# Block sums of the weights made by GpSimd in the front, and the second pair's first layer at two levels of Strassen

## The chip, the cores and the metric

The kernel runs on one core of a Trainium2 chip. A core has five engines with queues of their own: TensorE (PE, the matmuls, with PEld for its weight loads), VectorE (DVE), ScalarE (ACT), GpSimd (POOL) and SyncE (SP, which here only issues DMAs). Each takes its instructions in a fixed order and waits for semaphores of the others. Operands lie in SBUF, the on-chip memory of 128 partitions, matmul results in PSUM, in eight banks. Everything is computed in float32. The metric is the device time of one execution in microseconds.

## The reference

Two blocks follow each other. The first is linear attention with decay, in blocks of 64 positions, for 4 batches, 8 heads, 768 positions and 64 channels. Its result, with heads put beside each other, is `x` of 4 x 768 x 512. The second block mixes by a Fourier transform and adds a network of two layers:

```python
X = np.fft.fft(np.fft.fft(x, axis=1), axis=2)
u = x + np.real(X)
un = (u - mean(u)) / np.sqrt(var(u) + 1e-06)      # over the 512 channels
out = u + np.maximum(un @ w_ch1, 0.0) @ w_ch2     # 512 -> 2048 -> 512
```

The weights `w_ch1` and `w_ch2` are inputs, so whatever is made from them is made in every execution.

## The kernel before, in words

**Two stages.** In the front, batches go one after another through attention (`attn`, six chunks of 128 positions for each batch), the folds and matmuls of the Fourier transform and the normalisation (`fft_ln`). The transform uses its symmetries: VectorE adds and subtracts rows and mirrored rows (`fold_x`, `fold_a`, `fold_b`), TensorE multiplies the folded rows by small tables (L516, then `width`, L528 to L533), and `norm` makes the normalised tile. The mirrored rows come by indirect DMAs (gathers) that GpSimd issues in `mirror_a` and `mirror_b` (L439, L445, L452). GpSimd also scales keys (`kd`, L270) and the attention state (`st`, L319), takes the inverse root of the variance (`rs`, L550), and issues the indirect stores of rows to the output (L624).

A group is two tiles of 128 positions; there are twelve. The first four (`PLAIN`) go through both layers as plain matmuls, `mlp` (L635 and L649), woven between the front's work. The other eight (`LATE`) are transposed in blocks by VectorE into a tile with the tag `e` (L576), written to device memory (`utd`) and computed after the front, in four pairs of two groups each, with Strassen's method in Winograd's form: a product of 2 x 2 blocks with seven block products (`PRODUCTS`, L678) instead of eight. At two levels each of the seven is again made from seven products of quarters, 49 in all.

**The late stage.** Before it, VectorE makes the first level's block sums of both weights (`combine_weights`). `late` then runs the pairs in order. A first layer at one level is `first_layer` (L882, 7 x 8 x 2 matmuls with 256 columns), one at two levels is `deep_first` (L967, 49 x 4 matmuls with 128 columns). The second layer has two levels in every pair (`deep_second`, L1037). `DEEP` (L767) says how many pairs have a first layer at one level: two. At two levels a product needs block sums of a quarter of the weights: three or four tiles of 128 x 512, for each of seven weight blocks of either layer. GpSimd makes them while the one-level first layers run: `keep_sums` under pair 0 (those of the second weight, T1, T2, T4; the fourth is made in place of a quarter) and `keep_sums_w` under pair 1 (those of the first weight, S1 to S4). SP stores them in device memory (`s2.td`, `s2.sd`), and `load_three` brings three back ahead of each product. The tag `tx` with six slots holds a sum on its way out as well as on its way back. `place_sums_w` puts the fourth sum of each block of the first weight over a quarter that is no longer needed. In pair 0, `prepare_b` has the loads for the first two products issued behind the sums of the last turn, i = 6.

**What sets the order.** A planner in the compiler orders the instructions of each engine by program order and by when it takes their operands to be ready; it allots slots of a tag too. Program order comes from Python generators: each piece of work yields its estimated length, and `weave` draws from a second generator as much as a ratio allows. The last weave of the front takes the rest of `fr` (from batch 2's Fourier matmuls on, then batch 3) as its lead and the plain matmuls `back` beside it. `tc.keep_in_program_order` pins an instruction behind the one traced before it on its engine; instructions that are not pinned may step ahead. The front's tiles lie in pools that are closed after it, and the late stage's tiles are laid over them; of these `e` has two slots of 2 KB per partition.

In `in_step` the seven steps of each product alternate with those of the next, so that a product's end is interleaved with the start of the one behind.

## Time and profile before

| what | value |
|---|---|
| time, median of 3 runs | 798.99 us (798.94 to 800.15) |
| time of the profiled execution | 798.86 us |
| its span in the profile | 796.9 us |
| TensorE busy | 766.8 us, 96% |
| VectorE busy | 587.7 us, 74% |
| GpSimd busy | 195.6 us, 25% |
| sums by GpSimd under pair 0 | 433.08 to 471.83 us, 28 instructions |
| sums by GpSimd under pair 1 | 524.67 to 563.5 us, 28 instructions |
| pair 0, first layer from; second layer from | 428.71; 476.28 us |
| pair 1, first layer from; second layer from | 521.84; 568.46 us |
| pair 2, first layer from | 611.34 us |
| pair 3, first layer from | 698.88 us |

All times inside an execution count from the start of its span. A line of a group or of the timeline names the start, the duration, the engine, the line of the kernel, the operation, the tile written and those read, and in brackets the idle time ahead of it with what ended it. Matmuls in float32 have two records each. "SPq" is the queue of SP, a time there that of issuing DMAs.

### The profile page before, as it was taken

The page shows a single profiled execution, that of the slowest core. Times are in us where ns is not written, and L with a number is a line of the kernel's source. Part 1 is how long each engine was busy: PE and PEld are TensorE (multiplying, and loading weights), DVE is VectorE, ACT ScalarE, POOL GpSimd, SP SyncE. Part 2 cuts the span into 40 slices and gives each one's busy share as a digit, 9 for nine tenths or more (in the row PEclk, how much of TensorE's full clock was granted, in tenths as well). Part 3 has the DMA queues.
Part 4 walks back from the last instruction along what each step waited for, and adds up shares of the span by engine and source line. Part 5 has one row for each costly group of instructions (what it writes and reads, how often), then busy time and mean ns, then how long its engine had stood idle before and what let it go on. Part 6 is the DMA issues. An engine that isn't in the chain of part 4 may idle for free.

```text
span 796.9 us, 14576 instructions
## 1 busy us (share of the span) xinstructions
PE 766.8 (96%) x5616; PEld 647.2 (81%) x5616; DVE 587.7 (74%) x1148; ACT 216.7 (27%) x512; POOL 195.6 (25%) x196
## 2 busy tenths in 40 slices
PE   6989999999999999999999999999999999999996
PEld 5768776858675766777956889998999999999995
DVE  6899889685853573246598998769977699758983
ACT  3755443324431221221200221012210442024300
POOL 3233231011101020121003960279204101230021
PEclk9999999999999999999999999999999999999999
DMA  9979624238842037443232375345954555455432
GB/s 241 260 152 253 179 84 130 92 58 215 206 131 87 27 79 144 103 132 106 47 71 89 138 239 170 95 167 190 326 170 145 165 175 178 129 177 187 125 121 79
DMA packets 152331, 116.80 MB, mean 147 GB/s; under 512 B 113998, under 2 KB 113998, under 8 KB 152262
## 3 DMA queue, kind: packets, MB, share of 16 engines
q1 hardware_dynamic: 147120, 103.39, 46.1%
q0 software_dynamic: 2112, 6.69, 2.5%
q10 hardware_dynamic: 3030, 5.78, 2.1%
q8 instruction: 45, 0.74, 0.4%
q14 instruction: 24, 0.20, 0.1%
HBM read 83.58 MB, written 32.25 MB: 145 GB/s over the span
## 4 chain that ended last, share of the span: by engine, by line
PE 77%; DVE 10%; DMA 6%; issue 4%; ACT 2%; POOL 1%; SPq 0%; POOLq 0%; ACTq 0%; DVEq 0%
PE p L1037 21%; PE p L882 12%; PE p L967 11%; PE pm L649 9%; PE pm L635 8%; PE pa L516 3%; PE pa L332 3%; PE pa L298 3%; DMA raw<-in_moe_w_ch_dram 2%; DMA x<-xb,ix 2%; PE pa L328 2%; PE pa L274 1%; PE pa L315 1%; PE pa L348 1%; PE pa L279 1%
## 5 line engine op out<-in xcount | busy, mean ns | idle before, releaser
L635 PE MATMUL pm<-ut,w 128*128 128x256 f32 x512 | 118.8, 381 | 0.0
L649 PE MATMUL pm<-w,hr 128*128 128x512 f32 x256 | 115.7, 596 | 0.1
L635 PEld LDWEIGHTS pm<-ut,w 128*128 128x128 f32 x512 | 94.5, 190 | 14.0 <-issue 2.1
L649 PEld LDWEIGHTS pm<-w,hr 128*128 128x128 f32 x256 | 46.6, 190 | 49.3 <-issue 48.0
L1051 POOL TENSOR_TENSOR y<-y,u 128x512 f32<-128x512 f32 x12 | 18.8, 1570 | 199.1 <-DVE y L1060 156.7
L1037 PE MATMUL p<-tx,sx 128*128 128x128 f32 x416 | 54.9, 275 | 0.0
L1037 PEld LDWEIGHTS p<-tx,sx 128*128 128x128 f32 x416 | 50.6, 192 | 0.0
L882 PE MATMUL p<-ur,w 128*128 128x256 f32 x192 | 46.9, 379 | 0.1
L270 POOL TENSOR_TENSOR kd<-k,decay 128x512 f32<-128x512 f32 x20 | 22.2, 1109 | 95.9 <-PE pa L315 58.0
L1045 DVE TENSOR_TENSOR y<-p,y 128x128 f32<-128x128 f32 x92 | 25.6, 286 | 22.4 <-PE p L1037 15.7
L1043 ACT COPY y<-p 128x128 f32<-128x128 f32 x48 | 12.8, 266 | 104.1 <-PE p L1037 103.8
L882 PEld LDWEIGHTS p<-ur,w 128*128 128x128 f32 x192 | 36.3, 190 | 5.7 <-issue 0.5
L302 DVE TENSOR_TENSOR sc<-pa,decay 128x512 f32<-128x512 f32 x48 | 31.5, 683 | 8.5 <-PE pa L298 8.2
L1037 PE MATMUL p<-w,ha 128*128 128x128 f32 x288 | 37.4, 275 | 0.0
L298 PEld LDWEIGHTS pa<-qT,kT 64*128 64x128 f32 x384 | 26.0, 193 | 13.2 <-ACT qT L281 7.2
L1037 PEld LDWEIGHTS p<-w,ha 128*128 128x128 f32 x288 | 35.0, 192 | 0.2
L332 PE MATMUL pa<-sc,v 128*64 128x128 f32 x384 | 31.5, 282 | 3.8 <-DVE sc L302 3.7
L643 ACT ACTIVATE hr<-pm 128x256 f32<-128x256 f32 x44 | 16.7, 384 | 65.9 <-PE pm L635 65.6
L298 PE MATMUL pa<-qT,kT 64*128 64x128 f32 x384 | 30.7, 292 | 3.2 <-ACT qT L281 2.9
L549 POOL TENSOR_SCALAR ve<-mv 128x2 f32<-128x2 f32 x12 | 3.4, 286 | 122.6 <-DVE mv L546 122.6
L882 PE MATMUL p<-sx,w1s 128*128 128x256 f32 x128 | 32.9, 380 | 0.2 <-DVE sx L785 0.2
L332 PEld LDWEIGHTS pa<-sc,v 128*64 128x64 f32 x384 | 23.1, 137 | 11.4 <-DVE sc L302 5.3
(227 smaller groups left out, 1717.4 us busy)
## 6 DMA issues: line engine op xcount, KB each, us to landing
tx<-td SPq DMA_DIRECT2D x84, 256.0 KB, 2.9
raw<-in_moe_w_ch_dram SPq DMA_DIRECT2D x32, 512.0 KB, 5.4
tx<-sd SPq DMA_DIRECT2D x42, 256.0 KB, 2.7
sd<-tx SPq DMA_DIRECT2D x28, 256.0 KB, 2.0
k<-in_k_dram SPq DMA_DIRECT2D x24, 256.0 KB, 5.0
q<-in_q_dram SPq DMA_DIRECT2D x24, 256.0 KB, 6.0
v<-in_v_dram SPq DMA_DIRECT2D x24, 256.0 KB, 4.4
td<-tx SPq DMA_DIRECT2D x21, 256.0 KB, 2.0
```

The source lines that it names most:

```text
L270: nc.gpsimd.tensor_tensor(kd, kt, kpow, op=ALU.mult)
L298: mm(pss[hi][:, hp, :], lhsT=kT[HD[hi], hp, :], rhs=qT[HD[hi], hp, :], start=True, stop=True)
L302: nc.vector.tensor_tensor(t, pss[hi], decay[:, hi::2, :], op=ALU.mult)
L332: mm(po[HD[hi], hp, :], lhsT=vt[:, 2 * hp + hi, :], rhs=sc[hi][:, hp, :], start=(c == 0 and hp == 0), stop=(hp == HP - 1), skip_group_chec ...
L516: mm = nc.tensor.matmul(ps[:, n, :], lhsT=piece(a, i, n), rhs=cs[0:rows, a, i in (2, 3), n, :], start=(a == 0), stop=(a == 1))
L635: nc.tensor.matmul(ps, lhsT=w1[:, c, 128 * fc:128 * fc + 128], rhs=ut[:, c, :], start=(c == 0), stop=(c == KO - 1))
L649: nc.tensor.matmul(ps, lhsT=hr[(fc - f0) // 4][:, fc % 4, 128 * i:128 * i + 128], rhs=w2[:, fc, :], start=(fc == f0), stop=(fc == f1 - 1))
L882: nc.tensor.matmul(ps, lhsT=s2.A[a][:, kt, 128 * i:128 * i + 128], rhs=U[b][:, kt, :], start=(first and kt == 0), stop=(kt == 1), skip_gro ...
L967: nc.tensor.matmul(ps[:, 128 * i:128 * i + 128], lhsT=ab[m][0][:, 128 * i:128 * i + 128], rhs=ab[m][1], start=(start and i == 0), stop=Tru ...
L1037: nc.tensor.matmul(ps[:, 0:HM // 2], lhsT=ab[m][0][i], rhs=ab[m][1][:, i, :], start=(start and i == 0), stop=(i == HF // 2 - 1), skip_grou ...
L1045: V.tensor_tensor(o, ps[:, 0:HM // 2], o, op=ADD)
L1051: nc.gpsimd.tensor_tensor(o, y, u, op=ADD)
```

## The change

The sums of the weight blocks no longer hang on which first layer is running. One generator, `block_sums`, makes the four sums of a block and stores them.

For six blocks that are plain quarters of the weights and need no `combine_weights` (three of either layer: products 0, 1 and 5 of the first, 0, 1 and 6 of the second), `early_sums` makes them in the front: 24 instructions of GpSimd, each pinned, each followed by a store through SP to device memory. Three of the four tiles of a block take slots of `e`, and one a slot of its own, `ss`. `with_steps` puts one in wherever the last weave's lead has advanced by a 26th of its estimated length, at most one for each yield; what is left runs at the end. For the fourth sum of three blocks of the second weight, `place_sums_b` copies it from device memory into its place at the start of pair 0's first layer.

The other eight blocks (`later_sums`, 32 instructions) are made under pair 0's first layer: one block in each of the turns i = 0 to 5, two in the last, i = 6. With them, `DEEP` becomes 1, so that pair 1's first layer is computed at two levels. The keys' and queries' transposed tiles, `kT` and `qT`, get one buffer instead of two.

```diff
-        kT = new(at, [128, HP, C], "kT", bufs=2)
+        kT = new(at, [128, HP, C], "kT")
...
-        qT = new(at, [128, HP, C], "qT", bufs=2)
+        qT = new(at, [128, HP, C], "qT")
...
-    def keep_sums(k):
...
-    def keep_sums_w(k):
...
+    def block_sums(layer, k, quarters, shape, stage):
+
+        Q11, Q12, Q21, Q22 = quarters
+        S3, S2, S1, S4 = [stage[i](shape) if callable(stage[i]) else stage[i] for i in range(4)]
+        d = (s2.sd, s2.td)[layer][k] = [dram.tile(shape, F32, name=f"{'st'[layer]}d{k}{i}") for i in range(4)]
+        if layer == 0:
+            todo = ((3, S3, Q11, Q21, SUB), (1, S2, Q22, S3, SUB), (0, S1, S2, Q11, ADD), (2, S4, Q12, S2, SUB))
+        else:
+            todo = ((3, S3, Q22, Q12, SUB), (1, S2, S3, Q11, ADD), (0, S1, Q22, S2, SUB), (2, S4, Q21, S2, SUB))
+        for i, o, x, y, op in todo:
+            tc.keep_in_program_order(nc.gpsimd.tensor_tensor(o, x, y, op=op))
+            if o is not Q12:
+                nc.sync.dma_start(d[i], o)
+            yield 1.0
...
+    def early_sums():
...
+        blocks = [(0, 0, w1[:, k1, f1]), (1, 0, w2[:, b1, c1]), (0, 1, w1[:, k2, f1]), (1, 1, w2[:, b2, c1]),
+                  (0, 5, w1[:, k2, f2]), (1, 6, w2[:, b2, c2])]
+        for layer, k, t in blocks:
+            for d in block_sums(layer, k, (quarters_w, quarters_b)[layer](t), SHAPES[layer],
+                                [lambda s: new(ep, s, "e")] + [ep.tile(SHAPES[layer], F32, tag="ss", bufs=1, name=f"ss{layer}{k}")]
+                                + 2 * [lambda s: new(ep, s, "e")]):
+                yield d
...
+    def later_sums(i):
+
+        for layer, k in (((1, 3),), ((1, 2),), ((1, 4),), ((1, 5),), ((0, 3),), ((0, 4),), ((0, 2), (0, 6)))[i]:
+            q = (quarters_w, quarters_b)[layer]((s2.A, s2.B)[layer][PRODUCTS[k][layer]])
+            run(block_sums(layer, k, q, SHAPES[layer], [q[1] if layer else stage_tx] + 3 * [stage_tx]))
+
+    def place_sums_b():
+
+        for k in (0, 1, 6):
+            nc.sync.dma_start(quarters_b(s2.B[PRODUCTS[k][1]])[1], s2.td[k][3])
...
-    DEEP = 2
+    DEEP = 1
...
-            if j < min(DEEP, 2) and i < len(PRODUCTS):
+            if i < len(PRODUCTS):
                 if i == 0:
+                    place_sums_b()
                     tc.keep_in_program_order(nc.gpsimd.tensor_copy(s2.begun, h["a11"][:, 0, 0, 0:1]))
-                (keep_sums, keep_sums_w)[j](i)
+                later_sums(i)
...
+    def with_steps(gen, steps, each):
+
+        t = 0.0
+        for d in gen:
+            t += d
+            if t > each and next(steps, None):
+                t -= each
+            yield d
+        run(steps)
...
-    run(weave(fr, back, (t_back - t_half) / (t_rest - t_rest * t_half / t_back)))
+    t_last = t_rest - t_rest * t_half / t_back
+    run(weave(with_steps(fr, early_sums(), t_last / 26.0), back, (t_back - t_half) / t_last))
```

More of the change, by code (lines that the diff above doesn't have):

```diff
@@ L709, in quarters_b @@
         return [t[:, i:i + HF // 2, m:m + HM // 2] for i in (0, HF // 2) for m in (0, HM // 2)]
-    s2.td = []
+    s2.td, s2.sd = {}, {}
     s2.begun = wt.tile([128, 1], F32, name="begun")
-    def keep_sums(k):
-        pin = tc.keep_in_program_order
-        B11, B12, B21, B22 = quarters_b(s2.B[PRODUCTS[k][1]])
-        pin(nc.gpsimd.tensor_tensor(B12, B22, B12, op=SUB))
-        T1, T2, T4 = t = [new(s2.yp, [128, HF // 2, HM // 2], "tx", bufs=6) for _ in range(3)]
-        s2.td.append([dram.tile([128, HF // 2, HM // 2], F32, name=f"td{k}{i}") for i in range(3)])
-        for i, o, x, y, op in ((1, T2, B12, B11, ADD), (0, T1, B22, T2, SUB), (2, T4, B21, T2, SUB)):
-            pin(nc.gpsimd.tensor_tensor(o, x, y, op=op))
-            nc.sync.dma_start(s2.td[k][i], o)
@@ L725 @@
-    s2.sd = []
     def quarters_w(t):
         return [t[:, k, f:f + FH // 2] for f in (0, FH // 2) for k in range(2)]
-    def keep_sums_w(k):
-        pin = tc.keep_in_program_order
-        A11, A12, A21, A22 = quarters_w(s2.A[PRODUCTS[k][0]])
-        S3, S2, S1, S4 = [new(s2.yp, [128, FH // 2], "tx", bufs=6) for _ in range(4)]
-        s2.sd.append([dram.tile([128, FH // 2], F32, name=f"sd{k}{i}") for i in range(4)])
-        for i, o, x, y, op in ((3, S3, A11, A21, SUB), (1, S2, A22, S3, SUB), (0, S1, S2, A11, ADD), (2, S4, A12, S2, SUB)):
-            pin(nc.gpsimd.tensor_tensor(o, x, y, op=op))
-            nc.sync.dma_start(s2.sd[k][i], o)
+    def block_sums(layer, k, quarters, shape, stage):
[11 more added lines that the diff above has]
+            yield 1.0
@@ new lines @@
+    SHAPES = ([128, FH // 2], [128, HF // 2, HM // 2])
+    def early_sums():
+        k1, k2, f1, f2 = slice(0, 2), slice(2, 4), slice(0, FH), slice(FH, DFF)
+        b1, b2, c1, c2 = slice(0, HF), slice(HF, FO), slice(0, HM), slice(HM, DM)
+        blocks = [(0, 0, w1[:, k1, f1]), (1, 0, w2[:, b1, c1]), (0, 1, w1[:, k2, f1]), (1, 1, w2[:, b2, c1]),
[5 more added lines that the diff above has]
+                yield d
@@ new lines, in stage_tx @@
+    def stage_tx(shape):
+        return new(s2.yp, shape, "tx", bufs=6)
+    def later_sums(i):
[5 more added lines that the diff above has]
+            nc.sync.dma_start(quarters_b(s2.B[PRODUCTS[k][1]])[1], s2.td[k][3])
@@ L1139, in late @@
     def late():
-        for j in range(PAIRS):
-            if j < DEEP:
-                open_pair(j)
-                if j == 0:
-                    run(inputs(0))
-                first_layer(j)
-                if j + 1 < DEEP:
-                    in_step(second_layer(j) + [(inputs(j + 1), iter(()))])
+        open_pair(0)
+        run(inputs(0))
+        first_layer(0)
         in_step(second_layer(DEEP - 1) + [w for j in range(DEEP, PAIRS) for w in deep_pair(j)])
```

## The prediction

> **What bounds the kernel now.** I read the busy shares first, then the chain of waits, then the timelines of VectorE (DVE), GpSimd (POOL), TensorE (PE) and the DMA queue SP around the places that the change touches. On the page's first part:

> ```profile
> PE 766.8 (96%) x5616; PEld 647.2 (81%) x5616; DVE 587.7 (74%) x1148; ACT 216.7 (27%) x512; POOL 195.6 (25%) x196
> ```

> TensorE is the limit: some 30 us idle, two thirds of it at the two ends. Whatever makes it wait in between is paid in full, since its order is fixed. The chain of waits (start, us, what) of the last stage:

> ```profile
> 476.28 0.67 PE p L1037 x6
> ...
> 521.84 46.62 PE p L882 x216
> 568.46 0.67 PE p L1037 x6
> ...
> 611.34 0.89 PE p L967 x8
> ...
> 698.88 0.89 PE p L967 x8
> ```

> Read it as a calendar: second layer of pair 0 from 476.28, first layer of pair 1 (one level, L882) from 521.84, its second layer from 568.46, first layer of pair 2 (two levels, L967) from 611.34, of pair 3 from 698.88. Nothing but TensorE stands on the chain here.

> What the sums cost their neighbour shows in VectorE's timeline, during GpSimd's sums and after them:

> ```profile
> 437.11 1.48 DVE L896 TENSOR_TENSOR hs<-sv,ha 128x256 f32<-128x256 f32 x1
> 438.51 1.49 DVE L897 TENSOR_TENSOR hs<-ha,sv 128x256 f32<-128x256 f32 x1
> 439.92 0.41 DVE L894 TENSOR_TENSOR ha<-p,ha 128x256 f32<-128x256 f32 x1
> ...
> 478.38 0.42 DVE L896 TENSOR_TENSOR hs<-sv,ha 128x256 f32<-128x256 f32 x1
> ```

> The same operation takes 0.42 us alone and 1.48 beside a sum; L894, which reads PSUM, is untouched. So each sum holds one VectorE operation with two SBUF inputs by about 1.07 us. 28 sums run from 433.08 to 471.83: 1.384 us each.

> Then the place where GpSimd is idle and VectorE feeds TensorE directly (timelines of POOL, DVE, PE):

> ```profile
> 365.00 0.95 POOL L452 DMA_INDIRECT x<-xb,ix  x1 [0.30 <-issue]
> 389.11 0.22 POOL L549 TENSOR_SCALAR ve<-mv 128x2 f32<-128x2 f32 x1 [23.16 <-DVE mv L546]
> ...
> 370.08 0.42 DVE L475 TENSOR_TENSOR fe<-fe 128x256 f32<-128x256 f32 x1
> ...
> 370.56 0.59 PE L516 MATMUL pa<-cs,fe 128*128 128x193 f32 x2 [1.45 <-DVE fe L475]
> ```

> Eight folds of batch 3, all SBUF-only, run back to back from 367.18 to 370.50, and TensorE already waits 1.45 us for the last. GpSimd is free from 365.95 to 389.

> [...] the 256 KB stores of sums took 2.0, their loads 2.7 to 2.9.

> **Part 1, pair 1 at two levels.** From pair 0's second layer to pair 2's first layer now: 611.34 - 476.28 = 135.06. After: the stretch that leads from a second layer into a two-level first layer, 611.34 - 568.46 = 42.88, then a whole two-level pair, 698.88 - 611.34 = 87.54; together 130.42. Gain 4.64. In matmuls: one level issues 224 records at about 0.216 us (48.4), two levels 392 at 0.1117 (43.8). Its loads, its GpSimd inputs and `place_sums_w` come in the pattern that pair 2 shows behind pair 1, without a wait of TensorE.

> **Part 2, sums under pair 0's first layer.** 32 instead of 28: 433.08 + 32 x 1.384 = 477.4 instead of 471.8. Queue SP has the stores ahead of the loads of the second layer's T blocks:

> ```profile
> 468.84 3.33 SPq L723 DMA_DIRECT2D td<-tx  x3
> 472.26 2.79 SPq L759 DMA_DIRECT2D tx<-td  x6
> ```

> With the last store at about 477.8 the first load goes at 478.1 and lands at 480.8 to 481 (2.7 to 2.9), while TensorE wants T2 at 479.69 (first L1037 with tx). I take 1.2 us; ends 0 (a load put ahead of the stores) and 3 (the slowest landing, 5.5). VectorE ends four sums later, four times 1.07 behind; S2, now ready at 474.6, has 5 us of cover, S1 and S4 as much. `place_sums_b`'s three DMAs go at about 431, hidden behind 45 us of matmuls. Pair 1's 28 sums are gone, but TensorE lost nothing to them.

> **Part 3, 24 sums in the front.** Their GpSimd time, 24 x 1.3 = 31 us, fits into its idle time; their 24 stores too (DMA 30 to 40% busy, 2.0 us each). What counts is when they meet VectorE. A sum is pinned behind the GpSimd instruction before it in program order and behind nothing else. One step is due every 99.3/26 = 3.82 units. Summing the yields from batch 2's DFT on (where this weave starts): sums 1 to 5 fall in batch 2's DFT and norms, 6 to 15 in batch 3's attention, 16 right behind its last gathers, six (17 to 22) on the 21.6 units (1 + 3 + 9 + 5 x 1.4 + 1.6) before its first norm, 23 and 24 behind its first two norms' rs.
> - Batch 2, sums 1 and 2 right behind the gather of 263.24, mostly done when the folds begin at 266.56: 0.5 us (0 to 2.1).
> - Batch 2, sums 3 and 4 behind rs at 281.5 and 288.4, when VectorE turns to un. VectorE is gapless but for its waits on rs, up to sc, and TensorE waits 1.69 us for sc at 295.00. 2 x 1.07 = 2.1; I take 2.0 (0 to 3.2).
> - Attention of batch 3: VectorE's operations read PSUM; kd and st have 3 to 4 us until their matmuls. 0 (to 2).
> - Batch 3, sums 16 to 22: nothing but the staging slots spaces them, so they run from 366.0 as a bunch, over the folds. 16 is done when data lands at 367.15; 17 to 20 alternate with folds; 21 waits for 19's slot. Five of 17 to 22 before L475: 5 x 1.07 = 5.4 (2.1 with two, 7.5 with seven).
> - Sums 23 and 24: VectorE 2.1 later, against 2.02 us that it waits for TensorE at 428.9 after combining the weights: 0.3 (0 to 2.5).

> - Queues: the 24 stores take SP 24 x 0.36 = 9 us over 130 us. Behind a store that waits for its sum stand loads of q, k, v and stores of normalised tiles; SP is idle 30 of the 35 us before 386.8 and loads lead by a chunk, so 0. On TensorE everything behind L516 waits with it: the plain matmuls L635 stand in its order and can't step ahead, which is why 5.4 us of VectorE become 5.4 us of the kernel. Their cover would be an order in which some 25 of these records (0.216 us each) stood ahead of L516.

> kT and qT with one buffer cost nothing: in every chunk TensorE does L274, L279, then L298, so a chunk's copies come after the matmuls that read the one before. If chunks overlapped, a copy (0.59 us) would be waited for in each of 24. The buffers of the front lie 4 KB lower per partition and `ur` over another tile, so its load, now issued at 358, may wait longer; it is wanted at 428.7, and lands in 4 to 6: 0.

> Sum: 1.2 + 0.5 + 2.0 + 5.4 + 0.3 = 9.4 lost, 4.6 won: +4.8. Against the profiled execution (span 796.9, time 798.86) the span becomes 801.7 and the time 803.7; the median of the runs, 798.99, is 0.1 above that execution. I say 803.7.

> **Rivals.**
> - The bunch misses the folds (faster). One mechanism: the staging slots "e" are freed late enough to hold sums 17 to 22 until after 377, or the planner puts TensorE's plain matmuls ahead of L516. For it: six sums on two slots and one; against it: a slot comes back 2.3 us after its sum. Front 0, T2 1.2, gain 4.6: 795.5. It decides from where the front's losses fall under 3.4.
> - Cancelled: two or three sums meet the folds and the norms' cost half: 2.7 + 1.0 + 0.5 + 1.2 - 4.6 = +0.8, about 799.7. For it: VectorE's order may shift.
> - The slots block the queue: a sum without a slot holds up kd, st, rs behind it on GpSimd; the normalised tiles share "e", and SP issues stores in order, 12.8 us apart between its loads at 317.15 and 329.95. Two chunks late by 2 to 3 us each on top of +4.8: about 809. Against it: 3.82 units between sums there.
> - That pair 1 isn't computed at two levels: the code leaves no room; L967 would lack its 392 records.

> **Chances.** As forecast (801 to 807) 0.52; blocked queue 0.20; cancelled 0.14; faster 0.14. A measurement of this kernel tells about 0.2% (1.6 us) from no change. Faster 0.14, same 0.14, slower 0.72. The range 796 to 810 leaves out the best of the faster case (0.07) and the worst of the blocked one (0.1).

> **What would show it.** POOL sums bunched at the folds before the first norm of batch 3; folds of 1.4 us there; TensorE waiting about 7 us on L475 where it waited 1.45; pair 1 in 87.5 us; a wait of about 1 us for T2 in pair 0's second layer. Wrong if the folds stay at 0.42 us, if TensorE enters pair 0 less than 3.4 us later than 428.7, or if a new wait shows in the two-level pairs.

## The result, and the profile after

The changed kernel takes 819.73 us (median of 6 runs, 816.34 to 821.94) where the kernel before takes 799.12 beside it: a ratio of 1.0244, with a 95% interval of 1.0216 to 1.0272. The profiled execution has a span of 818.4 us, 21.5 more than before. The forecast of 803.7 had the right sign and under a quarter of the loss; its range ended at 810.

The page of the changed kernel: busy times, then the granted TensorE clock in 40 slices of 20.5 us.

```profile
PE 772.5 (94%) x5784; PEld 656.8 (80%) x5784; DVE 597.3 (73%) x1139; ACT 224.1 (27%) x512; POOL 202.3 (25%) x205
PEclk9999999999999699999899999999999999999998
```

TensorE has 168 records more, as forecast for one more first layer at two levels (392 against 224), and is idle 46 us instead of 30. The second row shows what the prediction has no term for: a slice with 0.6 of the full clock, from 266 to 286 us, and one with 0.8, from 389 to 409. In the kernel before each of the 40 shows a 9.

The chain of waits of the late stage (start, us, what):

```profile
503.26 1.92 PE p L902 x4
505.18 41.29 PE p L1058 x362
546.47 0.89 PE p L988 x8
...
634.01 0.89 PE p L988 x8
...
721.56 0.89 PE p L988 x8
```

Pair 1's first layer now has two levels (L988 from 546.47), and it and its second layer take 634.01 - 546.47 = 87.54 us, to the hundredth what the prediction read from pair 2. TensorE enters pair 0 at 451.20 instead of 428.71: the front alone lost 22.49 us. Ahead of 503.26 stands a stop of 2.88 us that the kernel before doesn't have; TensorE's timeline names what ended it:

```profile
503.26 1.92 PE L902 MATMUL p<-sx,w 128*128 128x256 f32 x4 [2.88 <-DVE ha L935]
```

Where the front lost its time: first the timelines of VectorE and TensorE in the kernel before at batch 2's second fold, then those of GpSimd, VectorE and TensorE in the changed one:

```profile
267.77 0.41 DVE L429 TENSOR_TENSOR fe<-fe 65x255 f32<-65x255 f32 x1
...
268.92 3.24 PE L516 MATMUL pa<-cs,fe 65*128 65x193 f32 x16 [0.33 <-DVE fe L470]
272.00 2.13 PE L516 MATMUL pa<-cs,fo 65*128 65x193 f32 x12
```

```profile
264.06 1.27 POOL L728 TENSOR_TENSOR e<-ss,w 128x512 f32<-128x512 f32 x1
270.80 2.80 POOL L728 TENSOR_TENSOR e<-w,ss 128x512 f32<-128x512 f32 x2
...
267.64 1.96 DVE L429 TENSOR_TENSOR fe<-fe 65x255 f32<-65x255 f32 x1
272.36 1.52 DVE L471 TENSOR_TENSOR fe<-fe 65x257 f32<-65x257 f32 x1
...
272.49 1.65 PE L516 MATMUL pa<-cs,fe 65*128 65x193 f32 x4 [4.04 <-DVE fe L470]
278.62 4.07 PE L516 MATMUL pa<-cs,fo 65*128 65x193 f32 x12
```

Six sums run from 264.06 to 273.6, and four fold operations take 1.5 to 2.0 us instead of 0.41. L516 comes at 272.49 instead of 268.92. And then twelve records of L516 take 4.07 us; before they took 2.13. The windows answer why (busy times of the engines; the number behind POOL's is the granted clock):

```profile
272.00:287.00 15.00, 14.05 (x54) 13.46 (x55) 5.08 (x12) 3.45 (x10) 1.60 (x2) 0.57 0.11 41
392.00:397.00 5.00, 5.00 (x15) 4.46 (x14) 5.00 (x15) 0.20 (x1) 0.00 (x0) 0.50 0.02 3
```

TensorE is busy nearly all the time, at half its rate. By 289.29, where the kernel before was at 279.79, the loss has gone from 3.57 to 9.50. The granted clock is at 0.50 from 271.35, inside the stop of 4.04 us, to 285.00, so it comes back only 12.5 us after the stop. Shorter stops bring it too (1.61 us in e18, below).

The other two places, in the timelines of SP, GpSimd, VectorE and TensorE; the first line is SP's load of the same `k` in the kernel before:

```profile
329.95 0.37 SPq L263 DMA_DIRECT2D k<-in_k_dram  x1
...
354.42 0.34 SPq L730 DMA_DIRECT2D sd<-e  x1
354.85 0.39 SPq L263 DMA_DIRECT2D k<-in_k_dram  x1
...
360.25 0.66 PE L274 MATMUL pa<-ident,k 128*128 128x128 f32 x4 [1.99 <-DMA k<-in_k_dram]
...
385.72 2.49 POOL L728 TENSOR_TENSOR e<-w,ss 128x512 f32<-128x512 f32 x2
386.74 2.03 DVE L426 TENSOR_TENSOR fe<-x,x 128x512 f32<-128x512 f32 x1 [3.46 <-DMA x<-xb,ix]
...
391.45 1.66 PE L516 MATMUL pa<-cs,fe 128*128 128x193 f32 x4 [5.51 <-DVE fe L475]
```

In batch 3's attention SP waits with the store of a sum until that sum is made, and the load of `k` stands behind it; before, it went out at 329.95. TensorE waits 1.99 us for it, and 3.55 us with the waits for `q` and those of the next chunk. At batch 3's fold the stop on L475 is 5.51 us instead of 1.45, and the half rate follows again.

The front's 22.5 us in the order of time:

| piece | us | read from |
|---|---|---|
| batch 2's second fold | 3.6 | L516 at 272.49 against 268.92 |
| half rate after it | 5.9 | 289.29 against 279.79, less the 3.57; a second wait of 0.46 is in it |
| batch 2's norms | 1.9 | L332 at 306.35 against 295.00, less the 9.50 |
| waits for `k` and `q` | 3.6 | 1.99 + 0.35 + 0.52 + 0.69 |
| batch 3's fold | 4.1 | 5.51 against 1.45 |
| half rate after it | some 3 | 0.50 from 391.45 to 397.64: half of these 6.2 us |

### The profile page after: what moved, and what is told of

Its sections match the earlier page's. It is cut to its first block, busy times and chain, and to the rows that moved or that the text cites. A ratio compares the mean times of both kernels' runs of the same rounds, so it can differ in the third digit from the quotient of the medians.

```text
span 818.4 us, 15006 instructions
## 1 busy us (share of the span) xinstructions
PE 772.5 (94%) x5784; PEld 656.8 (80%) x5784; DVE 597.3 (73%) x1139; ACT 224.1 (27%) x512; POOL 202.3 (25%) x205
## 4 chain that ended last, share of the span: by engine, by line
PE 71%; DVE 14%; DMA 6%; issue 5%; POOL 2%; ACT 2%; SPq 0%; POOLq 0%; DVEq 0%; ACTq 0%
PE p L1058 21%; PE p L988 16%; PE pm L649 10%; PE pm L635 8%; PE pa L516 3%; PE pa L298 3%; PE pa L332 2%; DMA x<-xb,ix 2%; PE pa L328 1%; DMA q<-in_q_dram 1%; DMA raw<-in_moe_w_ch_dram 1%; PE pa L274 1%; DVE hs L917 1%; PE pa L279 1%; PE pa L315 1%
## 5 line engine op out<-in xcount | busy, mean ns | idle before, releaser
L635 PE MATMUL pm<-ut,w 128*128 128x256 f32 x512 | 120.4, 385 | 0.9 <-DVE hr L641 0.9
L635 PEld LDWEIGHTS pm<-ut,w 128*128 128x128 f32 x512 | 95.8, 193 | 15.1 <-issue 1.9
L1058 PE MATMUL p<-tx,sx 128*128 128x128 f32 x400 | 52.8, 275 | 0.0
L1058 PEld LDWEIGHTS p<-tx,sx 128*128 128x128 f32 x400 | 48.7, 192 | 0.0
L997 DVE TENSOR_TENSOR ha<-p,ha 128x512 f32<-128x512 f32 x60 | 40.2, 687 | 9.7 <-PE p L988 9.5
L270 POOL TENSOR_TENSOR kd<-k,decay 128x512 f32<-128x512 f32 x20 | 22.9, 1144 | 87.7 <-PE pa L315 44.6
L1064 ACT COPY y<-p 128x128 f32<-128x128 f32 x48 | 12.8, 266 | 103.5 <-PE p L1058 103.1
L997 DVE TENSOR_TENSOR hs<-p,hs 128x512 f32<-128x512 f32 x39 | 26.3, 687 | 14.9 <-PE p L988 14.9
L298 PEld LDWEIGHTS pa<-qT,kT 64*128 64x128 f32 x384 | 26.1, 193 | 13.5 <-ACT qT L281 7.5
L332 PE MATMUL pa<-sc,v 128*64 128x128 f32 x384 | 31.6, 281 | 5.1 <-DVE sc L302 5.0
L298 PE MATMUL pa<-qT,kT 64*128 64x128 f32 x384 | 30.8, 292 | 3.4 <-ACT qT L281 3.2
L549 POOL TENSOR_SCALAR ve<-mv 128x2 f32<-128x2 f32 x12 | 3.3, 278 | 123.9 <-DVE mv L546 123.9
L988 PE MATMUL p<-sx,tx 128*128 128x128 f32 x264 | 33.9, 275 | 0.0
L332 PEld LDWEIGHTS pa<-sc,v 128*64 128x64 f32 x384 | 23.0, 137 | 12.8 <-DVE sc L302 6.9
```

Of the source, the lines that this page charges most:

```text
L270: nc.gpsimd.tensor_tensor(kd, kt, kpow, op=ALU.mult)
L298: mm(pss[hi][:, hp, :], lhsT=kT[HD[hi], hp, :], rhs=qT[HD[hi], hp, :], start=True, stop=True)
L332: mm(po[HD[hi], hp, :], lhsT=vt[:, 2 * hp + hi, :], rhs=sc[hi][:, hp, :], start=(c == 0 and hp == 0), stop=(hp == HP - 1), skip_group_chec ...
L635: nc.tensor.matmul(ps, lhsT=w1[:, c, 128 * fc:128 * fc + 128], rhs=ut[:, c, :], start=(c == 0), stop=(c == KO - 1))
L988: nc.tensor.matmul(ps[:, 128 * i:128 * i + 128], lhsT=ab[m][0][:, 128 * i:128 * i + 128], rhs=ab[m][1], start=(start and i == 0), stop=Tru ...
L997: V.tensor_tensor(o, p, o, op=ADD)
```

## The experiments

Eighteen kernels ran. Profiled executions without sums ahead of batch 2's first fold reach it at 259.6 to 263.6 us, so the last column gives the stretch from there to the end of the front. In the changed kernel, e2, e4 and e8 two sums stand ahead of that point, in e9, e12, e13 and e15 to e17 four to twelve; what these cost is not in the column. Each ratio is to executions of the kernel before that ran beside the kernel in question (their medians: 798.60 to 799.52), and it is taken from all of them, not from two medians.

| | what | median, us | ratio to before (95%) | span | front from batch 2's first fold |
|---|---|---|---|---|---|
| | before | 799.12 | | 796.9 | 167.6 |
| | after | 819.73 | 1.0244 (1.0216 to 1.0272) | 818.4 | 190.2 |
| e1 | no early sums | 797.79 | 0.9985 (0.9956 to 1.0014) | 796.0 | 167.2 |
| e2 | stores wait for no sum | 813.29 | 1.0158 (1.0124 to 1.0192) | 812.6 | 182.2 |
| e3 | before, one kT and qT | 798.51 | 1.0002 (0.9976 to 1.0028) | 797.3 | |
| e4 | 28 sums under pair 0 | 813.99 | 1.0181 (1.0163 to 1.0199) | 816.7 | 190.3 |
| e5 | sums in batch 3's attention | 810.84 | 1.0156 (1.0112 to 1.0200) | 809.6 | 179.1 |
| e6 | and stores by GpSimd | 805.82 | 1.0089 (1.0061 to 1.0117) | 803.9 | 175.9 |
| e7 | and the last block by VectorE | 801.92 | 1.0040 (1.0025 to 1.0054) | 801.0 | 175.9 |
| e8 | after, idle matmuls | 814.9, one run | | 812.7 | 185.0 |
| e9 | 12 sums in either attention | 802.99 | 1.0059 (1.0042 to 1.0075) | 800.2 | 169.1 |
| e10 | before, 2 idle sums | 799.27 | 1.0002 (0.9988 to 1.0016) | 797.2 | 169.0 |
| e18 | before, 3 idle sums | 802.08 | 1.0041 (1.0016 to 1.0065) | 800.8 | 172.8 |
| e11 | before, 4 idle sums | 805.41 | 1.0084 (1.0049 to 1.0119) | 802.8 | 175.3 |
| e12 | 4, 16, and 4 at the end | 806.29 | 1.0083 (1.0057 to 1.0109) | 803.7 | 174.3 |
| e13 | batch 3's keys by VectorE | 801.38 | 1.0021 (1.0004 to 1.0038) | 801.4 | 175.0 |
| e14 | before, keys by VectorE | 799.96 | 1.0008 (0.9987 to 1.0029) | 796.7 | 167.4 |
| e16 | as e13, sums denser | 800.83 | 1.0015 (0.9995 to 1.0034) | 800.8 | 174.9 |
| e15 | 8 and 16, ended early | 799.78 | 1.0006 (0.9985 to 1.0027) | 797.7 | 167.2 |
| e17 | and a slot of their own | 793.23 | 0.9919 (0.9903 to 0.9935) | 792.5 | 167.2 |

### Is it the early sums, and which part of them?

e1 takes the sums away and leaves their stores:

```diff
-            for d in block_sums(layer, k, ...):
+            for d in plain_stores(layer, k, ...):    # dma_start(d[i], quarters[0])
```

> The 24 sums of the front are left out; their 24 stores stay on SP and read plain quarters of the weights, so nothing waits for GpSimd. Theory A (sums hold folds of VectorE, TensorE stops, and its clock falls after a stop): TensorE leaves the front at 429 to 431 us as before, pair 0's first layer still loses 3.9, the two-level pair wins 4.6: 797 to 800 us. Theory B (the stores and the DMA traffic of the front cost most): the front stays 10 us or more late, 808 or more.

797.79 us, and from batch 2's first fold on the front is as before, at full clock. (In the first 120 us, where the changed kernel has no sums either, the clock is at 0.50 from 115.9 to 119.4, behind a stop of 2.25 us.) The whole of the front's loss hangs on the sums. The stop under pair 0 stays (2.87 us at 482.86, here without a lower clock), so it is a thing of its own.

e2 leaves the sums and frees the stores:

```diff
-                nc.sync.dma_start(d[i], o)
+                nc.sync.dma_start(d[i], Q11 if plain else o)
```

> All 24 sums stay in the front where they are; their stores read plain quarters of the weights instead of the sums and so wait for no sum. Theory A: the waits of TensorE for k and q of batch 3 (3.6 us) go, the fold stops and the low clock behind them stay: 814 to 817 us. Theory B: most of the loss goes, 799 to 804.

813.29. The waits for `k` and `q` are gone, and the stop at batch 3's fold is 1.15 us with no half rate after it, while batch 2's fold stops 5.27 us and half rate follows (L516 x16 in 5.52 us). The front is 8.0 us shorter than after. That is what SP's order costs with all that came with it, the late fold of batch 3 included. The two can't be told apart wholly: in e2 GpSimd's order at that fold is another as well, with the gathers of L452 (377.69) ahead of the indirect store that waits for `y` (382.62).

e3 gives the kernel before one buffer for `kT` and one for `qT`:

```diff
-        kT = new(at, [128, HP, C], "kT", bufs=2)
+        kT = new(at, [128, HP, C], "kT")
```

> The kernel before with one buffer each for kT and qT and nothing else. Theory A: no difference, 798 to 800 us. Rival C (the single buffers delay the attention): 802 or more.

No difference.

e4 leaves block (0, 6) unsummed, so that 28 sums stand under pair 0's first layer, as before:

```diff
-        for layer, k in (..., ((0, 2), (0, 6)))[i]:
+        for layer, k in (..., ((0, 2),))[i]:          # (0, 6): plain stores
```

> The changed kernel with the last block under pair 0 (four sums of the first weight's last block) left out: its four stores read a plain quarter; 28 sums as before. Theory A: TensorE's stop of 2.9 us at the end of pair 0's first layer goes with its slow clock: 815 to 817 us. Rival D (the order of the blocks, the two blocks in the last turn or the loads behind the stores make the stop): 819 or more.

The stop at the end of the first layer is gone, the front as slow as after. From TensorE's entry into pair 0 to pair 1's first layer it is 90.5 us (454.67 to 545.14) against 95.3 in the changed kernel. Four sums too many cost 4.8 us there.

### Moving the sums out of the folds

e5 has them fall into batch 3's attention alone:

```diff
-    fr = chain([att1, fft_ln(1)] + [front(b) for b in range(2, B)])
+    fr = chain([att1, fft_ln(1), front(2), with_steps(attn(3), early_sums(), 42.9 / 25.0), fft_ln(3)])
```

> All 24 sums of the front are traced inside batch 3's attention, where VectorE's operations read PSUM, and none over batch 2's folds and norms; stores stay on SP. Theory A: the stop at batch 2's folds (3.6), the slow clock behind it (5.9) and the wait at its norms (1.9) go, 11 us; SP is blocked in the attention as much or a little more: 806 to 811 us. Rival (the place of the sums does not matter, their number does): 816 or more.

e6 has GpSimd issue the stores (`queue.dma_start`, with `queue = nc.gpsimd` for the early sums):

> As the run before, and each early sum is stored through GpSimd's own queue behind the sum, so that SP waits for none. Theory A: the late loads of q and k go: 800 to 804 us. Rival (GpSimd, now with 24 issues of about 1 us more, holds up kd, st and the gathers): 806 or more.

e7 has VectorE sum block (0, 6) during pair 0's second layer:

> As the run before, and the last block under pair 0 is made by VectorE in pair 0's second layer, so that 28 sums run under the first layer. Theory A: the stop at its end goes, 3 to 4 us less than the run before: 797 to 800 us, at best 1% under the kernel before. Rival D: no less than the run before.

810.84, 805.82 and 801.92: each step takes away the waits that it was aimed at. In e5 batch 2 is as before, but `k` is late twice (1.95 and 2.10 us); in e6 it isn't; in e7 the stop under pair 0 is gone as well. What remains in e7, at 373.57, is a stop of 4.68 us ahead of L635, whose sixteen records then take 6.18 us (3.79 at 283.30 in the kernel before), and 2.12 us for a decayed key. That missed the 797 to 800 expected: 24 sums with their stores fill GpSimd from 311 to 377, and gathers and keys stand behind them.

### TensorE's clock by itself

e8 puts 36 idle matmuls of 128 x 128 ahead of the waiting L516 of the changed kernel:

```diff
+                    if (b, i, n, a) == (2, 0, 0, 1):
+                        fill = psum_a([128, 128])
+                        for _ in range(36):
+                            tc.keep_in_program_order(nc.tensor.matmul(fill, lhsT=ident, rhs=ident, start=True, stop=True))
```

> The changed kernel with 36 idle matmuls of 128x128 (8 us of TensorE) ahead of the matmul that waits for batch 2's second fold; the sums stay. Theory A (the clock falls because TensorE stops): no stop and a granted clock of 1.00 in the 15 us behind it, L516 at 0.165 us each there instead of 0.33; the span within 3 us of the changed kernel's, as some 4 us of plain matmuls come later and 6 us of slow clock go. Rival (the matmuls are slow there for another reason, such as the sums' traffic): the clock stays near 0.57 and the span grows by 4 us or more.

e8 tells little. The planner moved plain matmuls behind the idle ones, so a stop of 5.02 us stayed, and the half rate with it; only batch 3's stop was shorter (2.20 us), without a half rate.

So the stop was made on purpose in the kernel before, by idle additions of GpSimd on batch 2's second fold, two (e10), three (e18) and four (e11):

```diff
         tc.keep_in_program_order(tt(o[0:n, i, 0:DM], lo, hi, op=ALU.subtract))
+        for _ in range(4 if (b, a, i) == (2, 1, 0) else 0):
+            tc.keep_in_program_order(nc.gpsimd.tensor_tensor(new(ep, [128, 512], 'e'), w1[:, 0, 0:512], w1[:, 1, 0:512], op=ALU.add))
```

> The kernel before, with nothing of the change, and two idle additions of 128x512 by GpSimd (two quarters of a weight into a scratch tile that nothing reads) pinned onto batch 2's second fold. Each should delay one of VectorE's five operations ahead of the waiting L516 by about 1.07 us: TensorE's stop there grows from 0.3 to about 2.4 us. Theory A [...]: clock 1.00 in 269 to 287, the front 2 us longer, 800.5 to 801.5 us. Theory B (any stop is followed by slow matmuls): a clock of 0.6 to 0.8 there and 804 us or more.

> The kernel before with three idle additions by GpSimd on batch 2's second fold (e10 had two, e11 four). VectorE's first fold operation should be held till the third addition ends, so TensorE's stop should be 1.4 to 1.8 us. If the half rate comes only after a stop of over some 2 us: clock 1.00 and 800 to 801 us. If shorter stops bring it too: half-rate L516 (4 us for twelve) and 804 us or more.

> As e10, with four idle additions instead of two, so a stop of about 4.4 us, like that of the changed kernel. Theory A [...]: L516's twelve matmuls take about 4.1 us instead of 2.13, granted clock about 0.57 in 272 to 287, and the front is longer by the stop and about 6 us more: 807 to 810 us. Rival (the half clock of the changed kernel came from something else in it, its stores or its traffic, and the stop costs its own length only): clock 1.00, 803 us.

The timelines of GpSimd, VectorE and TensorE of e11:

```profile
262.91 5.00 POOL L427 TENSOR_TENSOR e<-w 128x512 f32<-128x512 f32 x4
...
265.17 3.29 DVE L426 TENSOR_TENSOR fe<-x,x 65x512 f32<-65x512 f32 x1 [3.48 <-DMA x<-xb,ix]
...
270.13 5.48 PE L516 MATMUL pa<-cs,fe 65*128 65x193 f32 x16 [2.81 <-DVE fe L470]
275.41 4.06 PE L516 MATMUL pa<-cs,fo 65*128 65x193 f32 x12
```

Nothing of the change is in this kernel, and its twelve records of L516 take 4.06 us too. So the half rate is the stop's doing, not that of stores or traffic, and "the stop costs its own length only" is out. The sizes I expected were off. Additions back to back (one each 1.25 us) don't alternate with VectorE's operations: one operation is held until the last of them has ended (3.29 us). Two additions were over when the fold began, so e10 gave no stop to judge by (0.34 us). Three gave 1.61 us and half rate all the same: L516 x12 in 4.07 us, full rate again from 281. Against e10, which kept the full rate, 2.5 us of a later L516 in e11 became 8.5 us by the next plain matmuls (284.04 against 275.50); about 6 us are the clock's. The bound of some 2 us that e18 was to try fell: 1.61 us was enough here.

Nor is it the length of the stop alone that decides. The traces of all twenty kernels show what goes with it. Within one execution the granted clock changes only at points a whole number of 3.41 us apart; in the changed kernel these are 271.35, 285.00, 390.81, 397.64, 503.45 and 506.87, in the kernel before 69.59 and 73.00. A stretch at 0.50 so lasts 3.41 us (before), 6.83 (after, from 390.81), 10.24 (e18) or 13.65 (after, from 271.35, and e11). In other executions the points lie elsewhere. Cut each trace into steps of 3.41 us between these points, leave out its first 45 us and its last 20, and compare how long TensorE was idle in a step with the clock in the next:

| kernel | stop, us | idle in the steps of 3.41 us that hold it | clock after them |
|---|---|---|---|
| after | 4.04 at 272.49 | 2.90 in the first | 0.50 |
| after | 2.58 at 306.35 | 1.70, then 0.87 | 1.00 |
| e4 | 2.57 at 310.16 | 2.57 | 0.50 |
| e1 | 2.87 at 482.86 | 1.19, then 1.69 | 1.00 |
| e10 | 1.68 at 293.72 | 1.68 | 0.50 |
| before | 1.69 at 295.00 | 1.57, then 0.12 | 1.00 |

The clock fell after all 24 steps at full clock with over 1.9 us of idle time, after none of the 3869 with under 1.4, and after 8 of the 32 between. So a stop that falls across one of these points can leave the clock alone where a shorter one inside a step lowers it. This is read from the traces; no run moved a stop against these points on purpose. What decides between 1.4 and 1.9 us stays open. So does the way back: the clock returned after one step without idle time, or sooner, everywhere but behind batch 2's second fold, where it took three or four such steps (three in the changed kernel, four in e11, one in e8). It fits that e18's thirteen executions, one kernel, have mean clocks from 0.987 to 0.998 and times from 808.29 to 797.88.

### Where the rest of the loss sat

e9 puts twelve sums into batch 2's attention and twelve into batch 3's:

```diff
-    fr = chain([..., front(2), with_steps(attn(3), early_sums(), 42.9 / 25.0), fft_ln(3)])
+    fr = chain([..., with_steps(attn(2), early_sums(0), 42.9 / 17.0), fft_ln(2),
+                with_steps(attn(3), early_sums(1), 42.9 / 16.0), fft_ln(3)])
```

> All 24 early sums stay, but twelve of them (the three blocks whose weights arrive first) are put into batch 2's attention and the other twelve into the first three quarters of batch 3's; the stores are issued by GpSimd; the last block (0,6) is summed by VectorE in pair 0's second layer, as in e7. Theory A (the change loses only where its sums stand ahead of a fold, of a norm, or of a decayed key or gather in a queue): no sum is left on a fold and GpSimd is free when batch 3's gathers are due, so TensorE leaves the front within 2 us of before (429 to 431), no stretch of the front has a granted clock under 0.95, and the 4.6 us that pair 1 gains are kept: 794 to 797 us, faster than before. Theory B (the early sums cost their VectorE time wherever they stand, some 24 x 1.07 us of which a part always reaches TensorE): 800 to 804 us.

e12 has four in batch 2's attention, sixteen in batch 3's (`42.9 / 21.0`) and four behind its last norm:

> As e9, with the early sums spread otherwise: block (0,0)'s four in batch 2's attention (the ones that cost nothing there in e9), sixteen in the first four fifths of batch 3's attention, and block (1,6)'s four after the last norm of batch 3, where GpSimd is idle. e9's loss lay in batch 2's attention alone (a decayed key behind a sum that waited 2.96 us for a slot: TensorE's stop of 5.13 us at 208.6). Theory A (place is all that the early sums cost): no stop over 2.5 us and no granted clock under 0.95 in the front, which TensorE leaves at 429 to 432; span 792 to 795, median 794 to 797. Theory B (the extra transfers and sums slow the front wherever they stand): 799 to 802 as e9 and e7.

Both missed. e9's twelve in batch 3's attention cost little: its stretch is 1.5 us longer than before, as e10's is (169.1 and 169.0), and in both the clock is at 0.50 for 3.41 us behind batch 2's norms. But batch 2's attention had a stop of 5.13 us at 208.63. In e12 that stop is gone; a key behind sums costs 3.93 us at 350.67, and the four late sums 5.05 us at 442.44, since they held slots of `e` that the last normalised tiles need; VectorE then waits 2.87 us for a store of `y` that SP issues only behind theirs.

e13 takes keys and states out of GpSimd's order in batch 3 and has twenty sums there; e14 does the same to the kernel before; e16 packs the twenty more densely (`42.9 / 31.0`):

```diff
-            nc.gpsimd.tensor_tensor(kd, kt, kpow, op=ALU.mult)
+            (nc.vector if b == 3 else nc.gpsimd).tensor_tensor(kd, kt, kpow, op=ALU.mult)
```

> As e12, but batch 3's decayed keys (L270) and state factors (L319) are multiplied by VectorE, so that none of them stands behind a sum on GpSimd, and block (1,6)'s four sums stand in batch 3's attention with the other sixteen instead of after the last norm. VectorE gets 5 x 0.68 and 4 x about 0.42 us more there, where it is busy for 19 of 65 us. Theory A (place and queue order are all that the early sums cost): no stop over 2.5 us in the front, which TensorE leaves at 429 to 432, and the 4.6 us of pair 1 are kept: span 792 to 795, median 794 to 797. Theory B (the front pays for the sums wherever they stand): 800 to 804.

> The kernel before, with batch 3's decayed keys and state factors multiplied by VectorE as in e13 and nothing else changed. GpSimd was no bound in the kernel before (it ends none of TensorE's waits there in batch 3's attention), so both theories expect no change: 798 to 800 us.

> As e13, with batch 3's twenty sums begun at smaller steps (a step per 1.4 units of the attention's cost instead of 1.7), so that they end earlier if GpSimd isn't full already. It is nearly full in e13 (20 x 2.15 us of 55), with some 8 us of waits for slots of e: the last sum should end 3 to 6 us earlier and the stop at 374.5 shrink to 0 to 3 us. Theory A: median 796 to 799. Theory B: 801 to 804.

The move alone is worth nothing (e14). In e13 one long stop is left, in the timelines of GpSimd and TensorE:

```profile
365.30 0.55 POOL L730 DMA_DIRECT2D td<-e  x1 [0.30 <-POOL e L728]
366.16 1.04 POOL L439 DMA_INDIRECT fo<-xa,ix  x1 [0.30 <-issue]
...
374.51 6.25 PE L635 MATMUL pm<-ut,w 128*128 128x256 f32 x16 [6.44 <-DVE y L661]
```

The gathers go out right behind the last store, with no wait of their own: GpSimd is full until then. Denser steps change nothing (e16: 174.9 against 175.0), so it was full, not unlucky.

e15 gives batch 2's attention eight of the sums, its keys to VectorE too, and leaves sixteen in batch 3's:

> As e13, with the decayed keys and state factors of batch 2 on VectorE as well, eight sums in batch 2's attention and sixteen in the first four fifths of batch 3's, so that the last sum ends some 5 us before the gathers L439 are due. Theory A (place is all that the early sums cost): no stop over 2.5 us and clock 1.00 at both folds, TensorE leaves the front at 429 to 433, span 792 to 796, median 794 to 798, so at or under before. Theory B (the front pays for them wherever they stand): 801 to 804, as e13.

799.78, no change against before. From batch 2's first fold to the end the front is as before (167.2), so sixteen sums in batch 3 cost nothing. The loss has moved to batch 2's attention, where the timelines of ScalarE, VectorE and TensorE show:

```profile
207.35 0.67 ACT L216 ACTIVATE e<-raw 128x512 bf16<-128x512 int16 x1 [5.77 <-DMA td<-e]
...
207.31 0.43 DVE L217 TENSOR_SCALAR e<-raw 128x512 uint16<-128x512 uint16 x1 [5.95 <-DMA td<-e]
...
208.55 1.12 PE L348 MATMUL pa<-ident,oT 128*128 128x128 f32 x4 [4.49 <-ACT oT L335]
```

The unpacking of a weight strip wants a slot of `e` that a sum's store still holds; ScalarE's copy of `oT` stands behind it. The same stop at the same place in e9 was therefore no matter of keys, as I had put it. e17 gives batch 2's sums one slot of their own:

```diff
+    def slot(shape, part):
+        return new(ep, shape, "e") if part else new(ep, shape, "es", bufs=1)
```

> As e15, with one slot of their own for the eight sums of batch 2's attention, so that no weight strip waits for a sum's store. Theory A (the sums cost only what they hold up by their place and their slots): no stop over 1.5 us from 200 to 245, batch 2's norms (L332) at 295 to 297 instead of 302.5, TensorE leaves the front at 428 to 431, and pair 1's 4.6 us are kept: span 791 to 794, median 792.5 to 796, faster than before. Theory B: 799 to 801 as e15.

793.23 us, 0.8% faster than before and 3% faster than the change as it was made. Its timeline of TensorE at batch 2's fold and norms, then its chain:

```profile
271.23 3.24 PE L516 MATMUL pa<-cs,fe 65*128 65x193 f32 x16 [0.44 <-DVE fe L470]
297.33 0.43 PE L332 MATMUL pa<-sc,v 128*64 128x128 f32 x2 [1.70 <-DVE sc L302]
```

```profile
520.94 0.89 PE p L991 x8
...
608.49 0.89 PE p L991 x8
```

Stops as in the kernel before (0.33 and 1.69 us), the front from batch 2's first fold 167.2 us. From pair 0's second layer (477.90) to pair 2's first (608.49) it is 130.59 us; the prediction said 130.42 against 135.06. TensorE reaches batch 2's first fold at 263.31, within what kernels without sums ahead of it show. All 24 sums are made, and no cost of theirs shows in the front: theory A of e9 to e17 holds, the front doesn't pay for the sums themselves. By the ratio e17 is some 6.5 us under the kernel before, nearly 2 more than pair 1 gives. Where these come from isn't shown: keys and states of batch 2 on VectorE were not tried in the kernel before, and the mean clocks of e17's six executions are 0.995 to 0.999, where those of the kernel before are 0.991 to 0.998.

## Why the prediction was right or wrong

**Part 1, the gain of 4.64: right.** 87.54 us for the new two-level pair, and 4.47 won in e17 where nothing hides it.

**Part 2, the loads of T2, 1.2: not paid.** No wait for T2 shows in any run with 32 sums. **"S2 ... has 5 us of cover, S1 and S4 as much": wrong**, and this term was set to nothing. TensorE stops 2.88 us, not for S2 but for VectorE's turn on a result (`ha`, L935), and its clock is at 0.50 from 503.45 to 506.87. The stretch from pair 0's second layer to pair 2's first is 135.39 us where 130.42 was said, so 5.0; e4 and e7 show that the four added sums are its cause.

**Part 3, batch 2's folds, 0.5: wrong.** The step that failed is the count "sums 1 to 5 fall in batch 2's DFT and norms". The first sum runs at 226.62, the second at 241.89, and eight have run when batch 2's folds are done, where I had two: the bunch that I put on batch 3's folds falls on these. The mechanism holds (six sums in a row, L516 3.57 later); the place was wrong.

**Batch 2's norms, 2.0: 1.85 measured, in part by luck.** The prediction has each of two sums hold one VectorE operation by 1.07 us. The sum at 290.97 does: L563 takes 1.71 us instead of 0.74. During the one at 298.25 VectorE stands still instead, since its transpose wants a slot of `e` whose sum this one is reading (before, it waited 0.83 us for `rs` there):

```profile
299.57 0.71 DVE L576 STREAM_TRANSPOSE e<-un 128x512 f32<-128x512 f32 x1 [1.75 <-POOL ss L728]
```

**Batch 3's folds, 5.4: near in size, wrong in cause for the most part.** The stop grew by 4.06. Of its eight folds only the first was held: L426 took 2.03 us instead of 0.69, beside the two sums from 385.72, so 1.3 us came the way that was forecast, by two sums and not by a bunch of seven. The other seven took 0.41 to 0.68 us. The gather L452 was issued only at 383.48, behind an indirect store that waited 3.38 us for `y`. In e2 the first fold takes 1.99 us as well, and the stop is 1.15 us: there the gathers stand ahead of that store, and between the attention's last product (L332) and the stop TensorE has work for 13.6 us, against 10.7 in the changed kernel. How much SP's late loads alone bring isn't shown.

**"Queues ... so 0": wrong.** TensorE's waits for `k` and `q` are 3.6 us; with what came along at batch 3's fold, e2 gives 8.0. I counted the issue times of the 24 stores and that loads lead by a chunk, but not that SP stands still while the store at its head waits for a sum that is pinned behind GpSimd's keys: 10 us apart where SP would need 0.4. The third rival had this in part (loads of two chunks late by 2 to 3 us each) at 0.20; it came with the folds, not in their place.

**"5.4 us of VectorE become 5.4 us of the kernel": wrong, and the largest miss.** The step counts a stop at its own length. In the changed kernel TensorE ran at half rate for 12.5, 6.2 and 3.6 us after three of its stops: that cost 5.9 us at batch 2's fold, some 3 at batch 3's, and about 2 (5.0 less the stop) at the end of pair 0's first layer, 11 in all. The prediction has no term for TensorE's clock. The kernel before shows the effect once ahead of its last 20 us, with 0.50 from 69.6 to 73.0 us behind stops of 1.21 and 0.40 us; its page, in slices of 20 us, hides it.

**`kT` and `qT` with one buffer, 0: right** (e3). "TensorE entering pair 0 less than 3.4 us later" was named as what would make the prediction wrong; it came 22.5 us later, which no case held. A reading that nothing hangs on is off as well: 14.3 of TensorE's 30.1 idle us lie in the first and last 20 us, so half and not two thirds.

## What to carry to other kernels

A stop of the engine that sets the time has to be priced with what can follow it: here a stop that left TensorE idle for over 1.9 us in one step of 3.41 us brought 3.4 to 13.7 us at half rate, which cost up to 6 us more. Work for an idle engine is not free because the engine has time: ask for each piece what stands behind it in that engine's order, behind its store in the DMA queue's, and who else takes its staging slots; with these three cleared, the same 24 sums showed no cost (e17). Place it by when it runs in the trace, not by counted steps.
